# Packed attention and two mixtures of experts: two of four etm copies in batches 1 to 3 on VectorE

## The chip, the cores and the metric

One core of one Trainium2 chip runs the whole program in one launch. The metric is the device time in microseconds, the median of three runs. All stage times in this document are microseconds from the start of one profiled execution's span.

## What is computed

The reference, cut to what matters (S = 576 tokens, 4 batches, 8 heads, 32 packed queries, head width 64):

```python
def sm_attn(qq, kk, vv):
    s = scale * np.matmul(qq, kk.transpose(0, 1, 3, 2))
    a = np.exp(s - np.max(s, axis=-1, keepdims=True))
    a = a / (np.sum(a, axis=-1, keepdims=True) + 1e-09)
    return np.matmul(a, vv)

p_packed = sm_attn(p, k, v)                  # 32 packed queries read all tokens
out = sm_attn(q, p_packed, p_packed)         # the tokens read the 32 results
x = out.transpose(0, 2, 1, 3).reshape(2304, 512)

p = domain_probs / domain_probs.sum(-1)      # first mixture, 4 experts
x = sum(p[:, e:e+1] * (np.maximum(x @ w1[e], 0) @ w2[e]) for e in range(4))

logits = x @ phi                             # second mixture, 8 experts of 4 slots
d = softmax(logits, axis=0); slot_input = d.T @ x
slot_out = relu(slot_input @ w1) @ w2        # per expert
result = softmax(logits, axis=1) @ slot_out
```

## The kernel before

The program has three stages. A **head** loads and attends batch 0 and prepares the projected weights. The **main loop** makes 128 steps ("slots"), 32 for each batch; a slot multiplies one expert's 128 hidden features by all 576 tokens of its batch. The **tail** does the second mixture; it streams weights from memory.

Inside the main loop, the first-mixture work of batch b runs with the attention of batch b+1 threaded between. In each slot the kernel calls its steps in a fixed order written out by hand, "FGMLSAP": turn the hidden tile of the slot before (`flip_h`), make the next merged weights (`make_g`), multiply (`mm1`), take logits, one step of the softmax generator, one step of each attention generator, and the accumulations of the batch before. The engines run their own queues in this order; semaphores between them set the rest.

The attention of one batch is two generators, group 0 and group 1 of four heads each; group 1 starts nine slots after group 0 (`OFF1`). Each `yield` in `attention` ends its part of a slot. The steps around the change:

- L332 to L334: VectorE normalizes the exponentials `ex` of the packed scores (128 partitions by 576 tokens) and turns them by 32 by 32 blocks into `et`, where each of four heads has 32 partitions and each token block of 32 has 32 columns.
- L337 to L344: for each half of the token blocks (nine of eighteen), four copies bring `et` into the **block form** `etm`. Head h goes to its own 32 partitions, to parity h % 2, and into columns 0 to 31 or 32 to 63 of each 64-wide row; the other half of every row stays zero, so that one product serves two heads. The source is one run of 288 values per partition, the destination nine rows of 32 at a pitch of 64.
- L348 to L357, one slot later: TensorE multiplies the token blocks of v by `etm`, 18 matmuls per half (the trace has two records for each), parity 0 and parity 1 in turn, into the accumulator `pv`. Parity 0 reads the copies of heads 0 and 2, parity 1 those of heads 1 and 3.
- L361: ScalarE moves `pv` to `gl`, GpSimd spreads it to `pkt` (L370), and the second attention (`sb`, L381) reads `pkt`.

There is one `etm` buffer in the main loop. So the second half's copies wait for the first half's products. Per batch there are four sets of four copies, called here **g0h0, g0h1, g1h0, g1h1** (group, half); batches 1 to 3 have twelve sets, 48 copies.

What else stands in the queues near them: ScalarE drains each half of a hidden tile from PSUM with a Relu (L481, `ht`), and the merged weights by a cast (L458). VectorE turns the hidden tile (L487, `hn`) and makes the low part of the merged weights (L459), whose end frees the PSUM bank that the next product takes. GpSimd multiplies the turned tile by the domain probabilities (L488), multiplies in the attention softmax (L390, L399), makes low parts (L414) and issues the loads of q, k, v and p (L136, L143). Four PSUM banks serve `h`, `g`, `sa`, `sb` and `pv` in turn (`mm_ps`).

Of the kernel before, what the change touches and what calls it, by code (L numbers as in the profile page):

```python
# [18 lines left out]
def tile_packed_attention_moe_softmoe(  # L19
# [15 lines left out]
    pe, act, dve, pool, sp = nc.tensor, nc.scalar, nc.vector, nc.gpsimd, nc.sync  # L35
# [60 lines left out]
    def mm_ps(name, keep=None):  # L96
        i = (turns["mm"] + 1) % 4
        while i in kept.values():
            i = (i + 1) % 4
        turns["mm"] = i  # L100
        if keep is not None:
            kept[keep] = i
        return ps_mm[i].tile([128, 512], F32, tag="mm", name=name)
# [178 lines left out]
    def attention(b, g, feeds, ptb, pkb, etb, tmp, gp):  # L282
# [3 lines left out]
        def feed(key):  # L286
            if key in feeds:
                due.append(feeds[key])
# [48 lines left out]
        for hf in range(2):  # L337
            for h in range(4):
                r = slice(32 * h, 32 * h + 32)
                act.copy(  # L340
                    etb[hf % len(etb)][r, h % 2, :, 32 * (h // 2) : 32 * (h // 2) + 32],
                    et[r, HB * hf : HB * hf + HB, :],
                )
            yield  # L344
            vn = qkv_t.pop(("v", b, g, hf))
            if pv is None:
                pv = mm_ps(f"pv{bg}", bg)
            for x in range(HB):  # L348
                for par in range(2):
                    pe.matmul(  # L350
                        pv[64 * par : 64 * par + 64, :64],
                        vn[:, x, :],
                        etb[hf % len(etb)][:, par, x, :],
                        start=(hf == 0 and x == 0),
                        stop=(hf == 1 and x == HB - 1),
                        tile_position=(0, 64 * par),
                    )  # L357
            feed(f"k{hf}")
            if hf == 0:
                yield  # L360
# [59 lines left out]
    def start_attention(b, g):  # L420
        feeds = {}
        nb, ng = (b, 1) if g == 0 else (b + 1, 0)

        def later(src, nm, hf, bb, gg):
            return lambda: load_half(src, nm, bb, gg, hf)

        for hf in range(2):
            feeds[f"q{hf}"] = later(q, "q", hf, b, g)
            if nb < NB:
                feeds[f"k{hf}"] = later(k, "k", hf, nb, ng)  # L430
                feeds[f"v{hf}"] = later(v, "v", hf, nb, ng)
        if nb < NB:
            f = feeds["k0"]
            feeds["k0"] = lambda: (load_p(nb, ng), f())
        return attention(b, g, feeds, pt, pkt[:, g], [etm], att_tmp, pool)
# [335 lines left out]
    with tc.manual_schedule():  # L771
# [58 lines left out]
        def head_tmp(tag, name):  # L830
            if tag == "kt":
                return ht_pool.tile([128, S], F32, tag="ht", name=name)
            return spare[tag]

        gens = {
            "0": attention(0, 0, {}, pt, pkt[:, 0], [etm, et_x[0]], att_tmp, dve),
            "1": attention(
                0, 1, {}, pp1, pkt[:, 1], [et1, et_x[1]], head_tmp,
                pool if GP1 == "pool" else dve,
# [38 lines left out]
        for sl in range(nslot + 1):  # L878
# [3 lines left out]
            b, i = divmod(n, NU)  # L882
# [250 lines left out]
        for so, (d0, dw) in zip(sos, PARTS):  # L1133
            project(1, CHUNK // dw, dw, [(so, 0, dw)])
            h = slice(d0, d0 + dw)
# [56 lines left out]
```

## Time and profile before

| | |
|---|---|
| median of three runs | 533.5 us (532.25 to 533.76) |
| the profiled execution's own time | 533.42 us |
| its span in the trace | 531.6 us |
| TensorE, busy in the span | 493.3 us (93%) |
| VectorE, ScalarE, GpSimd, busy | 292.7, 236.0, 248.3 us |
| the 48 copies on ScalarE, one | 0.428 us |

Read it as follows. The profile's chain of waits goes back from the last instruction through whatever ended last. Its shares tell where a change of engine can matter. The timeline shows, for one stretch, each engine's instructions merged by group: start, length, engine, line, tile, count, and in square brackets how long the engine sat idle before the group and what ended that. An idle time of TensorE inside the main loop is time that the program could lose; an idle time of the other engines is not.

### The profile page before, as it was taken

How to read it: one execution, taken by the hardware profiler on the slowest of the kernel's cores; microseconds unless marked ns; L12 is line 12 of the kernel's file. 1: busy time of each engine (PE TensorE's matmuls, PEld its weight loads, DVE VectorE, ACT ScalarE, POOL GpSimd, SP SyncE). 2: the span in 40 equal slices, each digit the busy share in tenths (PEclk: the TensorE clock that was granted, in tenths of full speed). 3: DMA queues.
4: the chain of work that ended last, by engine and by line, in shares of the span. 5: the costliest groups of instructions: out<-in, count | busy, mean ns of one | idle time of the engine just before them, and what ended most of it. 6: DMA issues, size and time to landing. Idle time of an engine off the chain costs nothing.

```text
span 531.6 us, 12920 instructions
## 1 busy us (share of the span) xinstructions
PE 493.3 (93%) x5404; PEld 349.0 (66%) x5404; DVE 292.7 (55%) x539; ACT 236.0 (44%) x539; POOL 248.3 (47%) x310
## 2 busy tenths in 40 slices
PE   6898999999999999999999999999999987998883
PEld 5776877778765677787557778865678864323232
DVE  6265566656677656567775755676554553412031
ACT  3847555664552447465424474652355430111031
POOL 8502356487752367875326567842455540300000
PEclk9899999999999999999999999999999998898996
DMA  8999135433440353443304423443359449999998
GB/s 276 367 373 315 46 103 191 161 126 127 140 144 3 106 190 105 148 157 104 104 1 150 146 82 129 150 170 109 121 187 390 173 167 373 408 408 407 373 317 282
DMA packets 66713, 104.06 MB, mean 196 GB/s; under 512 B 4368, under 2 KB 50192, under 8 KB 66656
## 3 DMA queue, kind: packets, MB, share of 16 engines
q1 hardware_dynamic: 62640, 93.10, 49.5%
q0 software_dynamic: 3232, 9.75, 6.0%
q8 instruction: 42, 0.69, 0.5%
q10 hardware_dynamic: 784, 0.39, 0.3%
q14 instruction: 15, 0.12, 0.1%
HBM read 98.52 MB, written 4.72 MB: 194 GB/s over the span
## 4 chain that ended last, share of the span: by engine, by line
PE 66%; DMA 11%; DVE 8%; ACT 8%; issue 3%; POOL 3%; SPq 1%; POOLq 0%; DVEq 0%; ACTq 0%
PE h L477 32%; PE sl L648 7%; PE lg L504 6%; PE g L447 5%; DMA ck<-in_moe_w_dram 5%; DMA hn<-in_moe_w_dram 3%; ACT etm L340 3%; PE pv L350 3%; PE sb L301 3%; PE sa L301 2%; DMA k<-in_k_dram 2%; PE w2t L255 1%; PE si L1027 1%; PE o L1153 1%; POOL hn L488 1%
## 5 line engine op out<-in xcount | busy, mean ns | idle before, releaser
L477 PE MATMUL h<-a,g 128*128 128x288 f32 x1536 | 226.2, 302 | 2.5 <-POOL a L414 1.6
L477 PEld LDWEIGHTS h<-a,g 128*128 128x128 f32 x1536 | 208.0, 188 | 28.3 <-issue 22.3
L488 POOL TENSOR_TENSOR hn<-hn,dp_sb 128x576 f32<-128x576 f32 x128 | 151.5, 1190 | 123.0 <-DVE hn L487 118.7
L481 ACT ACTIVATE ht<-h 128x288 f32<-128x288 f32 x256 | 103.7, 412 | 149.4 <-PE h L477 149.0
L487 DVE STREAM_TRANSPOSE hn<-ht 128x576 f32<-128x576 f32 x128 | 96.6, 760 | 55.1 <-ACT ht L481 55.0
L459 DVE TENSOR_TENSOR g<-g,g 128x512 fp32r<-128x512 f32 x64 | 41.1, 684 | 26.5 <-ACT g L458 26.5
L648 PE MATMUL sl<-hn,dpt 32*32 32x512 f32 x1152 | 48.1, 597 | 1.5 <-DVE dpt L607 1.2
L458 ACT CAST g<-g 128x512 fp32r<-128x512 f32 x64 | 34.3, 588 | 21.0 <-PE g L447 21.0
L504 PE MATMUL lg<-ht,wphi 128*32 128x288 f32 x512 | 37.8, 412 | 0.0
L447 PE MATMUL g<-w,gl 64*32 64x512 f32 x512 | 35.7, 601 | 0.2 <-DVE tacc L666 0.2
L648 PEld LDWEIGHTS sl<-hn,dpt 32*32 32x32 f32 x1152 | 21.0, 103 | 21.5 <-issue 11.1
L504 PEld LDWEIGHTS lg<-ht,wphi 128*32 128x32 f32 x512 | 13.5, 109 | 32.7 <-issue 25.5
L350 PE MATMUL pv<-etm,v 128*64 128x64 f32 x468 | 20.0, 232 | 7.1 <-ACT etm L340 4.0
L414 POOL TENSOR_TENSOR a<-a,a 64x576 fp32r<-64x576 f32 x14 | 19.9, 1425 | 9.6 <-ACT a L413 8.9
L350 PEld LDWEIGHTS pv<-etm,v 128*64 128x64 f32 x468 | 17.1, 144 | 11.1 <-ACT etm L340 5.7
L340 ACT COPY etm<-et 32x288 f32<-32x288 f32 x52 | 22.2, 428 | 2.4 <-DVE et L334 1.2
L1120 PE MATMUL so<-hn,tacc 128*32 128x384 f32 (+1 forms) x96 | 19.5, 487 | 2.5 <-DMA hn<-in_moe_w_dram 2.4
L382 DVE STREAM_TRANSPOSE nat<-sb 128x288 f32<-128x288 f32 x14 | 6.8, 483 | 25.4 <-PE sb L301 25.4
L255 PE MATMUL w2t<-ident,hn 128*128 128x128 f32 x128 | 19.3, 301 | 1.4 <-ACT hn L260 1.4
L666 DVE TENSOR_TENSOR tacc<-sl,tacc 128x512 f32<-128x512 f32 (+2 forms) x32 | 15.3, 544 | 9.4 <-PE sl L648 9.4
L260 ACT COPY hn<-w2t 128x512 f32<-128x512 f32 x32 | 17.4, 588 | 6.8 <-PE w2t L255 6.8
L255 PEld LDWEIGHTS w2t<-ident,hn 128*128 128x128 f32 x128 | 15.8, 154 | 5.9 <-ACT hn L260 3.8
(179 smaller groups left out, 483.6 us busy)
## 6 DMA issues: line engine op xcount, KB each, us to landing
w<-in_moe_w_dram SPq DMA_DIRECT2D x32, 1024.0 KB, 5.3
ck<-in_moe_w_dram SPq DMA_DIRECT2D x44, 512.0 KB, 8.9
hn<-in_moe_w_dram SPq DMA_DIRECT2D x40, 512.0 KB, 9.9
hn<-in_moe_w_dram SPq DMA_DIRECT2D x16, 384.0 KB, 8.4
q<-in_q_dram POOLq DMA_DIRECT2D x12, 288.0 KB, 3.2
k<-in_k_dram POOLq DMA_DIRECT2D x10, 288.0 KB, 3.3
v<-in_v_dram POOLq DMA_DIRECT2D x10, 288.0 KB, 3.2
out_dram<-ob SPq DMA_DIRECT2D x7, 384.0 KB, 4.4
```

The costliest lines, as they stand in the source:

```text
L255: pe.transpose(ps[:, 128 * dc : 128 * dc + 128], w2_row(ft, e)[:, 128 * dc : 128 * dc + 128], ident,)
L340: act.copy(etb[hf % len(etb)][r, h % 2, :, 32 * (h // 2) : 32 * (h // 2) + 32], et[r, HB * hf : HB * hf + HB, :],)
L350: pe.matmul(pv[64 * par : 64 * par + 64, :64], vn[:, x, :], etb[hf % len(etb)][:, par, x, :], start=(hf == 0 and x == 0), stop=(hf == 1 an ...
L447: pe.matmul(pss[g][32 * ((c + 2 * g) % 4) : 32 * ((c + 2 * g) % 4) + 32, :], gl[b % 2][r, c, :], t[r, c], start=True, stop=True, tile_posi ...
L458: act.copy(hi, pss[g])
L459: dve.tensor_tensor(out=lo, in0=pss[g], in1=hi.bitcast(F32), op=ALU.subtract)
L477: pe.matmul(ps[:, :HS], gg[:, l, g, e % 2, fs], r[:, ts], start=(g == 0 and t == 0), stop=(g == 1 and t == 2),)
L481: act.activation(out=ht[:, ts], in_=ps[:, :HS], func=AF.Relu)
L487: dve.transpose(out=own, in_=unturned.pop((n, kf, e)).rearrange("p (x t) -> p x t", t=32))
L488: pool.tensor_tensor(out=own, in0=own, in1=dp_sb[:, n // NU, :, e].unsqueeze(2).to_broadcast([128, NBLK, 32]), op=ALU.mult,)
L504: pe.matmul(lg_t[b, pr][32 * c : 32 * c + 32, :HS], wphi[:, 2 * i + kf, 32 * e : 32 * e + 32], ht_t[n, kf, e][:, HS * hf : HS * hf + HS], ...
L648: pe.matmul(pss[f][c : c + 32, :], dpt[r, x, :], hn[r, p0 : p0 + NU, x, 2 * ep : 2 * ep + 2].rearrange("p n e k f -> p n (e k f)"), start= ...
```

## The change

Heads 2 and 3 of every set go to VectorE in batches 1 to 3. Batch 0, in the head, keeps all its copies on ScalarE. Nothing else is edited: 24 copies move, none is added.

```diff
         for hf in range(2):
             for h in range(4):
                 r = slice(32 * h, 32 * h + 32)
-                act.copy(
+                (dve.tensor_copy if b and h > 1 else act.copy)(
                     etb[hf % len(etb)][r, h % 2, :, 32 * (h // 2) : 32 * (h // 2) + 32],
                     et[r, HB * hf : HB * hf + HB, :],
                 )
```

On VectorE, batch 1, group 1, first half (g1h0): `et` is the turned softmax, `hn<-ht` the hidden tiles of two slots, `g` the low part of the merged weights.

```order
 L334 STREAM_TRANSPOSE et_1328<-ex_1190 128x576 [waits DVE_49]
 L487 STREAM_TRANSPOSE hn<-ht_1_2_1305 128x18x32 [waits Activation_49]
+L340 COPY etm<-et_1328 32x9x32 [waits DVE_49]
+L340 COPY etm<-et_1328 32x9x32
 L487 STREAM_TRANSPOSE hn<-ht_1_3_1332 128x18x32 [waits Activation_49]
 L459 TENSOR_TENSOR g_1_1356<-g_1_0_1357,g_1_1356 128x512 [waits Activation_49]
```

Two copies now stand between the two hidden-tile transposes, and ahead of the low part of the weights.

On VectorE, the same batch and group, second half (g1h1): `a` is the turned result of group 0's second softmax.

```order
 L487 STREAM_TRANSPOSE hn<-ht_0_0_1379 128x18x32 [waits DMAHW6_49,DMAHW5_49,DMAHW7_49,DMAHW0_49,Activation_49]
 L404 STREAM_TRANSPOSE a_1444<-nat_1268 128x576 [waits Pool_49]
+L340 COPY etm<-et_1328 32x9x32 [waits PE_49] x2
 L487 STREAM_TRANSPOSE hn<-ht_0_1_1427 128x18x32 [waits Activation_49]
 L487 STREAM_TRANSPOSE hn<-ht_1_0_1452 128x18x32 [waits Activation_49]
```

The two copies stand behind a transpose that waits for GpSimd, and wait themselves for TensorE, which must have finished the first half's products.

On ScalarE, the set g1h0 again: `nat` is the exponential of group 0's second softmax, `g` the cast of the merged weights.

```order
 L394 ACTIVATE nat_1268<-nat_1268 128x576 [waits Pool_49]
 L340 COPY etm<-et_1328 32x9x32 [waits DVE_49]
-L340 COPY etm<-et_1328 32x9x32 x3
+L340 COPY etm<-et_1328 32x9x32
 L458 CAST g_1_1356<-g_1_0_1357 128x512 [waits PE_49]
 L458 CAST g_1_1356<-g_1_1_1358 128x512 [waits PE_49]
```

Two copies instead of four stand ahead of the two casts.

## Rows read from the trace of the kernel before

**Rows 1.** The page's chain that ended last, share of the span by line
```profile
PE h L477 32%; PE sl L648 7%; PE lg L504 6%; PE g L447 5%; DMA ck<-in_moe_w_dram 5%; DMA hn<-in_moe_w_dram 3%; ACT etm L340 3%; PE pv L350 3%; PE sb L301 3%; PE sa L301 2%; DMA k<-in_k_dram 2%; PE w2t L255 1%; PE si L1027 1%; PE o L1153 1%; POOL hn L488 1%
```

**Rows 2.** Timeline (start, length, work, [idle before <- releaser]), batch 1, g0h1
```profile
78.67 1.29 DVE L459 TENSOR_TENSOR g<-g,g 128x512 fp32r<-128x512 f32 x2 [1.49 <-ACT g L458]
79.00 3.45 PE L477 MATMUL h<-a,g 128*128 128x288 f32 x24
...
81.33 1.79 ACT L340 COPY etm<-et 32x288 f32<-32x288 f32 x4
...
82.72 1.71 PE L350 MATMUL pv<-etm,v 128*64 128x64 f32 x36 [0.27 <-ACT etm L340]
```

**Rows 3.** Timeline, batch 1, g1h0
```profile
101.06 1.40 DVE L487 STREAM_TRANSPOSE hn<-ht 128x576 f32<-128x576 f32 x2
...
101.96 1.77 ACT L340 COPY etm<-et 32x288 f32<-32x288 f32 x4
...
102.80 1.86 PE L477 MATMUL h<-a,g 128*128 128x288 f32 x12
103.76 1.07 ACT L458 CAST g<-g 128x512 fp32r<-128x512 f32 x2
104.38 1.29 DVE L459 TENSOR_TENSOR g<-g,g 128x512 fp32r<-128x512 f32 x2 [1.92 <-ACT g L458]
...
105.12 1.27 PE L350 MATMUL pv<-etm,v 128*64 128x64 f32 x36 [0.46 <-DVE g L459]
```

**Rows 4.** Timeline, batch 1, g1h1
```profile
106.32 3.45 PE L477 MATMUL h<-a,g 128*128 128x288 f32 x24
...
108.17 0.78 DVE L404 STREAM_TRANSPOSE a<-nat 128x576 f32<-128x576 f32 x1 [0.62 <-POOL nat L399]
...
108.66 1.79 ACT L340 COPY etm<-et 32x288 f32<-32x288 f32 x4
...
110.05 1.71 PE L350 MATMUL pv<-etm,v 128*64 128x64 f32 x36 [0.28 <-ACT etm L340]
```

**Rows 5.** Timeline, batch 1, g0h0
```profile
68.22 6.64 PE L477 MATMUL h<-a,g 128*128 128x288 f32 x48
...
73.73 1.40 DVE L487 STREAM_TRANSPOSE hn<-ht 128x576 f32<-128x576 f32 x2
73.84 1.79 ACT L340 COPY etm<-et 32x288 f32<-32x288 f32 x4
74.54 2.33 POOL L488 TENSOR_TENSOR hn<-hn,dp_sb 128x576 f32<-128x576 f32 x2 [1.87 <-DVE hn L487]
...
75.23 1.71 PE L350 MATMUL pv<-etm,v 128*64 128x64 f32 x36 [0.37 <-ACT etm L340]
```

**Rows 6.** Timeline, group 0's scores in batch 2, and the same place in batch 3
```profile
188.99 0.78 DVE L292 STREAM_TRANSPOSE k<-k 128x576 f32<-128x576 f32 x1 [2.14 <-DMA k<-in_k_dram]
...
189.91 1.21 PE L301 MATMUL sa<-k,pt 128*128 128x288 f32 x4 [0.47 <-ACT ht L481]
...
292.73 1.21 PE L301 MATMUL sa<-k,pt 128*128 128x288 f32 x4 [0.79 <-DVE k L292]
```

**Rows 7.** VectorE's groups by form: line, tiles, shapes, count, busy, mean ns
```profile
L186 DVE TENSOR_REDUCE dps<-dp_sb 128x72 f32<-128x288 f32 x1 | 0.5, 452 | 0.0
```

**Rows 8.** Timeline, GpSimd and VectorE before g0h0 of batch 1
```profile
71.49 1.19 POOL L488 TENSOR_TENSOR hn<-hn,dp_sb 128x576 f32<-128x576 f32 x1 [2.80 <-DVE sm L330]
...
71.70 1.29 DVE L332 TENSOR_SCALAR ex<-ex,sm 128x576 f32<-128x576 f32 x1
```

**Rows 9.** Timeline, batch 1, GpSimd's spread of pv and the product behind it
```profile
116.61 1.93 POOL L370 COPY pkt<-gl 32x32 f32<-32x32 f32 x8
...
118.89 1.13 PE L301 MATMUL sb<-q,pkt 128*128 128x288 f32 x4
```

**Rows 10.** The tail: SyncE's timeline, then a stretch (length, engines' busy, PEclk, DMA share, GB/s)
```profile
437.46 15.55 SPq L749 DMA_DIRECT2D hn<-in_moe_w_dram  x16
...
470.00:480.00 10.00, 10.00 (x76) 2.84 (x72) 2.05 (x4) 1.60 (x4) 0.00 (x0) 1.00 1.03 409
```

## The prediction

> **What bounds the kernel now.** I read the chain of waits first. TensorE's products carry most of it, but ScalarE's etm copies have 3% of it by themselves and pv, the product that reads them, another 3% [rows 1]. A copy that is on the chain is one that TensorE waits for. So the timeline around each of the twelve sets comes next, and in each I look at two things: when TensorE ends the work in front of pv, and when pv really flows. A pv that nothing holds takes 1.27 us for its 36 records [rows 3]. Where the fourth copy comes late it takes 1.71 [rows 2, 4, 5]: two records run after the third copy, and the other 34 after the fourth, so 0.44 us of that group is a hidden wait. The idle time in brackets and this 0.44 are together what a set costs TensorE.
>
> **The change, part by part.** *What moves.* Twelve sets give up two ScalarE copies each. Four take 1.79 us [rows 2], one 0.45, so two take 0.90 and heads 0 and 1 are ready 0.9 us earlier than the set is today. *The price on VectorE.* No row shows this copy there. [...] A copy that VectorE could do faster is bounded below by half the column rate: L332 shows 576 columns done 0.31 us after GpSimd's multiply ended (71.70 + 1.29 against 71.49 + 1.19) [rows 8], so 288 columns could take 0.16 to 0.31. I take 0.46, the row with the same column count and no wait in it, so 0.92 a pair. Upward the bound is a copy that must first wait for a whole GpSimd multiply of 1.19 us: 1.19 + 0.31 = 1.50, 3.0 a pair. No reason excludes it; it is a rival below.
>
> *g0h1, batch 1.* TensorE ends h at 79.00 + 3.45 = 82.45; pv starts 0.27 later and loses 0.44 inside, 0.71 in all [rows 2]. VectorE's copies stand right behind L459, which ends at 79.96, and their wait for the first half's product is long over: done by 80.88. ScalarE's two end at 81.33 + 0.90 = 82.23. Both are ahead of 82.45, so all **0.71** goes. What is late next is h itself.
>
> *g0h1, batches 2 and 3.* The same 0.71 appears there, but little of it lasts. Group 0's second score product needs the second half of k. In batch 2 its turned form is ready at 188.99 + 0.78 = 189.77, after a 2.14 us wait for the load, and sa starts at 189.91; so the shift ends at about **0.10** [rows 6]. In batch 3 sa already waits 0.79 us for that transpose: TensorE would only wait longer, **0** [rows 6]. The load hangs on the one before it, whose issue hangs on work ahead of this set, so the change doesn't move it. In batch 1 I let the gain stand: k there arrives early enough.
>
> *g1h0, three times.* Here pv waits 0.46 us not for the copies but for the PSUM bank that L459 frees; L459 waits for ScalarE's cast, and the cast for the four copies [rows 3]. With two copies gone the casts start 0.88 earlier, 102.88, and the first ends about 103.5. VectorE must be free by then: its first transpose ends about 101.8, two copies take it to 102.7, the second transpose to about 103.4. So L459's first half runs 103.5 to 104.2, and the bank is free before h ends at 102.80 + 1.86 = 104.66. pv follows h at once: **0.46** each. The cover that hides the added 0.92 on VectorE is its old idle time of 1.92 us before L459; a pair beyond 1.8 us would give the whole gain back (101.8 + 1.8 + 0.75 + 0.70 = 105.05). Queued behind the copies are the second transpose and with it GpSimd's next multiply, about 0.5 us later than today; what GpSimd does next waits for sums behind L459, which come earlier.
>
> *g1h1, three times.* h ends at 106.32 + 3.45 = 109.77, pv starts 0.28 later and loses 0.44: 0.72 [rows 4]. ScalarE's two copies end at 108.66 + 0.90 = 109.56. VectorE's stand behind L404, which ends 108.95 today, so 109.87 if nothing moved; but L404 waits for GpSimd's L399, which waits for sums behind L459, and L459 is 0.85 earlier by the step before. TensorE's own frame is 0.46 earlier, so the pair ends about 0.3 before h does. **0.72** each. The pattern of these two sets reads alike in batches 1, 2 and 3.
>
> *g0h0.* In batch 1, h ends at 74.86, pv loses 0.37 + 0.44 = 0.81 [rows 5]. VectorE's copies stand behind a transpose that ends about 74.47, so the last ends at 75.39, against 75.64 for ScalarE's fourth today: pv flows at 75.41 in place of 75.68, **0.27**. In batches 2 and 3 the accumulation of the batch before stands between copies and pv, so the copies are ready long before, and VectorE waits for TensorE there: **0**, and nothing lost.
>
> *Sum:* 0.27 + 0.71 + 0.10 + 3 x (0.46 + 0.72) = 4.62 us.
>
> *Does it reach the end?* The tail is bound by weight loads: 1.03 of the DMA engines' time at 409 GB/s. SyncE issues the long run of loads from 437.46, as the last accumulations of the main loop free their buffers [rows 10]. So the stream starts earlier by what TensorE gains, with the same bytes behind it, and I carry the gain through in full. Against the profiled execution, 533.42 - 4.62 = 528.8 us. That execution lies 0.08 below the median of the runs, so no correction.
>
> [...] L332 shows VectorE standing still until GpSimd's multiply ends, at 72.68, and then doing 576 columns in 0.31 us [rows 8]. [...]
>
> **The rivals.**
>
> *Copies and multiplies exclude each other.* As mechanism of this kernel: VectorE's first copy gets in, GpSimd's multiply goes next, the second copy waits 1.19 us for it. In g0h0 of batch 1 the multiply starts at 74.54, when the copies do [rows 5]: the second ends at about 76.2, a loss of 0.5. In g1h0 L459 slips to about 104.15 and pv to 104.9: 0.22 left. In g1h1 about 0.5 is left. In g0h1 GpSimd is idle or done in time. So -0.5 + 0.71 + 0.10 + 3 x 0.72 = 2.5, 530.9 us. For it: L332. Against: it needs the faster form of the copy. 0.15.
>
> *GpSimd becomes late.* After g1h1, sb needs pkt, which GpSimd ends at 118.54, and sb starts at 118.89 [rows 9]. If GpSimd's queue doesn't move up, only 0.35 of group 1's 1.18 stays, and with batches 2 and 3 taken like batch 1: 0.27 + 0.71 + 0.10 + 3 x 0.35 = 2.1, 531.3 us. Against: that queue waits, two steps before, for a ScalarE cast that itself stands behind the copies. 0.10.
>
> *Slower.* Each of the two copies waits for a multiply, 3.0 us a pair. Then g0h0 of batch 1 loses 1.8; g0h1 gains about 0.3; in g1h0 L459 slips past its old time by 1.1, and g1h1's copies, behind it, come 2.6 late in all: -1.8 + 0.3 - 3 x 2.6 = -9.3, 542.7 us. It decides from about 1.7 us a pair, 0.85 a copy, where the losses in group 1 and g0h0 pass the gain of g0h1. For it: VectorE is the busier engine of the two. Against: GpSimd has one multiply per slot, and no two free ones for one pair. 0.06.
>
> *It does not do what it says:* the gaps close, but another wait of TensorE opens by as much before the loads start, and under 1.6 us is left, near 532.5. For it: batches 2 and 3 already show one such place. 0.07. *More than forecast:* copies near 0.3 us and no exclusion give g0h0 of batch 1 its whole 0.81, and the k loads of batches 2 and 3 come forward; 4.62 + 0.54 + 0.6 + 0.7 = 6.5, 526.9 us. 0.07.
>
> **How the numbers follow.** The forecast has 0.55; its own range is 527.9 to 529.8, from pairs between 0.4 and 1.2 us. The range from 527.2 to 532.0 takes in the two rivals near 531 and leaves out the slower case and parts of the last two. About 0.3%, 1.6 us, is what a measurement of this kernel can tell from no change. Faster by more: 0.55 + 0.07 + 0.11 + 0.08 = 0.81. Within: 0.07 and what is left of the two middle rivals, 0.13. Slower: 0.06.
>
> **What would show it.** Right: etm on VectorE at about 0.46 us; in the six group 1 sets and g0h1 pv in one run of about 1.27 us with little idle before it; L459 of g1h0 about 0.9 earlier against the h in front of it; sa of batch 3 waiting longer for k, about 1.5 us; the hn loads of the tail issued near 432.9. Wrong: VectorE copies over 0.85 us, or a copy that ends when a GpSimd multiply does; pv still in 1.71; sb waiting for pkt; a tail that starts earlier and ends when it did.

## The result and the profile after

The changed kernel takes 527.86 us (median of 4, 526.99 to 529.14) where the kernel before took 532.88 in the same comparison (4, 531.61 to 533.76): a ratio of 0.9916, with a 95% interval from 0.9889 to 0.9942. A second comparison, on another chip, gave 528.46 against 532.12, 0.9930 [0.9908, 0.9952]. Forecast were 528.8 us and a gain of 4.62 us; the profiled execution of after took 528.35 us, 5.07 below that of before (533.42). The forecast holds. Times and gains below are in us.

The page's chain by line no longer names the copies, which had 3% [rows 1]; pv has gone from 3% to 2%, and the load of k from 2% to 4%:

```profile
PE h L477 35%; DMA hn<-in_moe_w_dram 7%; PE lg L504 6%; DMA ck<-in_moe_w_dram 6%; PE g L447 6%; PE sl L648 5%; DMA k<-in_k_dram 4%; PE sb L301 3%; PE sa L301 2%; PE pv L350 2%; PE w2t L255 1%; PE o L1153 1%; PE pw L241 1%; DVE tacc L666 1%; POOL hn L488 1%
```

The copies of after by engine, batches 1 to 3 (count, shortest/median/longest in ns, first and last start), and who waited for them:

```profile
L340 ACT COPY etm<-et x24: 413/432/432, 73.7 to 308.5; 32x288 f32<-32x288 f32 x24
L340 DVE COPY etm<-et x24: 444/447/451, 74.4 to 308.4; 32x288 f32<-32x288 f32 x24
...
  PEld pv L350: 1.4, 7
  PE pv L350: 0.2, 1
```

A copy takes 0.447 us on VectorE, with 7 ns between the shortest and the longest. Asked the same way, the trace of before has TensorE waiting 2.0 us for copies, 7 times, and its weight loads 5.5 us, 14 times; in after it is 0.2 us once, and 1.4 us 7 times.

The timeline of after at the four sets of batch 1 (start, length, work, idle before and releaser), in the order g0h0, g0h1, g1h0, g1h1, and then the spread of pv and the product behind it; it answers to [rows 2 to 5] and [rows 9]:

```profile
74.37 0.92 DVE L340 COPY etm<-et 32x288 f32<-32x288 f32 x2
74.42 1.19 POOL L488 TENSOR_TENSOR hn<-hn,dp_sb 128x576 f32<-128x576 f32 x1 [1.87 <-DVE hn L487]
...
74.96 0.30 PE L350 MATMUL pv<-etm,v 128*64 128x64 f32 x2 [0.23 <-DVE etm L340]
...
75.44 1.23 PE L350 MATMUL pv<-etm,v 128*64 128x64 f32 x34 [0.18 <-ACT ht L481]
...
78.73 3.46 PE L477 MATMUL h<-a,g 128*128 128x288 f32 x24
79.72 0.92 DVE L340 COPY etm<-et 32x288 f32<-32x288 f32 x2
...
82.11 1.27 PE L350 MATMUL pv<-etm,v 128*64 128x64 f32 x36
...
100.79 0.91 DVE L340 COPY etm<-et 32x288 f32<-32x288 f32 x2
100.84 1.19 POOL L488 TENSOR_TENSOR hn<-hn,dp_sb 128x576 f32<-128x576 f32 x1 [0.54 <-DVE hn L487]
...
101.75 1.86 PE L477 MATMUL h<-a,g 128*128 128x288 f32 x12
...
102.44 1.29 DVE L459 TENSOR_TENSOR g<-g,g 128x512 fp32r<-128x512 f32 x2
...
103.55 1.27 PE L350 MATMUL pv<-etm,v 128*64 128x64 f32 x36
104.75 3.44 PE L477 MATMUL h<-a,g 128*128 128x288 f32 x24
...
107.05 0.93 DVE L340 COPY etm<-et 32x288 f32<-32x288 f32 x2
...
108.12 1.27 PE L350 MATMUL pv<-etm,v 128*64 128x64 f32 x36
...
114.64 1.94 POOL L370 COPY pkt<-gl 32x32 f32<-32x32 f32 x8
...
116.52 1.13 PE L301 MATMUL sb<-q,pkt 128*128 128x288 f32 x4
```

In g0h1, g1h0 and g1h1 all 36 records of pv run in 1.27 us with no bracket: no idle time that the profile shows stands before them. In g1h0 L459 starts 0.69 after h does (102.44 against 101.75), where it was 1.58 in before (104.38 against 102.80 [rows 3]), 0.89 earlier against it. Only g0h0 still runs in two pieces, 2 and 34. GpSimd's eight copies of the spread end at 116.58 (the profile's spans of GpSimd are rough) and sb starts without idle time at 116.52, where it started 0.35 after their end [rows 9]: GpSimd came forward by 1.96, TensorE by 2.37, and sb does not wait for it. The 0.35 to spare there are used up.

The timeline of after where group 1's second score product needs k, in batches 2 and 3; it answers to [rows 6], whose products are group 1's too and not group 0's, as their heading has it. In batch 3 the two lines of SPq and POOL ahead are SyncE's load of w, the factors of the next merged weights, and GpSimd's issue of the first part of k; the second part is issued at 284.79:

```profile
186.48 0.78 DVE L292 STREAM_TRANSPOSE k<-k 128x576 f32<-128x576 f32 x1 [2.02 <-DMA k<-in_k_dram]
...
187.41 1.21 PE L301 MATMUL sa<-k,pt 128*128 128x288 f32 x4 [1.08 <-DVE k L292]
...
277.05 14.46 SPq L169 DMA_DIRECT2D w<-in_moe_w_dram  x2
277.51 0.54 POOL L143 DMA_DIRECT2D k<-in_k_dram  x1
283.71 0.78 DVE L292 STREAM_TRANSPOSE k<-k 128x576 f32<-128x576 f32 x1 [1.76 <-DMA k<-in_k_dram]
...
284.79 0.58 POOL L143 DMA_DIRECT2D k<-in_k_dram  x1 [2.44 <-DVE k L292]
...
287.86 0.78 DVE L292 STREAM_TRANSPOSE k<-k 128x576 f32<-128x576 f32 x1 [2.06 <-DMA k<-in_k_dram]
...
288.79 1.21 PE L301 MATMUL sa<-k,pt 128*128 128x288 f32 x4 [1.41 <-DVE k L292]
```

TensorE waits 1.08 and 1.41 us there, against 0.47 and 0.79 [rows 6]. The first part of k, issued at 277.51, 0.46 behind a 1 MB load of w, is turned at 283.71, 6.2 us later; the second part's issue waits for that (2.44).

SyncE's timeline in the tail, and a stretch of it (length, busy time of TensorE, its weight loads, VectorE, ScalarE and GpSimd, granted clock of TensorE, DMA share, GB/s); it answers to [rows 10]:

```profile
432.21 14.35 SPq L749 DMA_DIRECT2D hn<-in_moe_w_dram  x16
...
465.00:475.00 10.00, 10.00 (x76) 2.84 (x72) 2.06 (x4) 1.60 (x4) 0.00 (x0) 1.00 1.03 410
```

The stream of loads starts 5.25 earlier than in before and runs at 410 GB/s, where it was 409, and the execution takes 5.07 less.

### The profile page after: what moved, and what is told of

Its sections match the earlier page's. It is cut to its first block, busy times and chain, and to the rows that moved or that the text cites. A ratio compares the mean times of both kernels' runs of the same rounds, so it can differ in the third digit from the quotient of the medians.

```text
span 526.6 us, 12931 instructions
## 1 busy us (share of the span) xinstructions
PE 490.3 (93%) x5404; PEld 347.9 (66%) x5404; DVE 303.9 (58%) x563; ACT 226.4 (43%) x515; POOL 248.4 (47%) x310
## 4 chain that ended last, share of the span: by engine, by line
PE 65%; DMA 17%; DVE 7%; issue 4%; ACT 4%; POOL 2%; SPq 1%; POOLq 0%; DVEq 0%; ACTq 0%
PE h L477 35%; DMA hn<-in_moe_w_dram 7%; PE lg L504 6%; DMA ck<-in_moe_w_dram 6%; PE g L447 6%; PE sl L648 5%; DMA k<-in_k_dram 4%; PE sb L301 3%; PE sa L301 2%; PE pv L350 2%; PE w2t L255 1%; PE o L1153 1%; PE pw L241 1%; DVE tacc L666 1%; POOL hn L488 1%
## 5 line engine op out<-in xcount | busy, mean ns | idle before, releaser
L459 DVE TENSOR_TENSOR g<-g,g 128x512 fp32r<-128x512 f32 x64 | 41.1, 685 | 20.6 <-ACT g L458 20.6
L301 PE MATMUL sa<-k,pt 128*128 128x288 f32 x56 | 17.2, 434 | 3.0 <-DVE k L292 2.9
L350 PE MATMUL pv<-etm,v 128*64 128x64 f32 x468 | 17.1, 225 | 2.6 <-ACT etm L340 1.3
L350 PEld LDWEIGHTS pv<-etm,v 128*64 128x64 f32 x468 | 15.1, 138 | 5.1 <-issue 2.0
```

What stands on the lines that cost most here:

```text
L301: pe.matmul(ps[:, :HS], lhs[:, j, :], t[:, :, j, :], start=(j == 0), stop=(j == 1))
L350: pe.matmul(pv[64 * par : 64 * par + 64, :64], vn[:, x, :], etb[hf % len(etb)][:, par, x, :], start=(hf == 0 and x == 0), stop=(hf == 1 an ...
L459: dve.tensor_tensor(out=lo, in0=pss[g], in1=hi.bitcast(F32), op=ALU.subtract)
```

## How the stages are compared

The head does not take the same time in every execution: group 0's second score product of batch 1, which stands ahead of every moved copy in the loop, starts between 61.47 and 63.44 in the fourteen profiles of this study. In the six where it starts at 63.25 to 63.44, those of before and after among them, TensorE's granted clock in the stretch from 51 to 56 is 0.66 (in before it is 0.50 from 53 to 55, in after from 52 to 54); in the other eight it is 1.00, and the product starts at 61.47 to 62.30. The stretch in after and in the kernel with group 1 alone (columns as in the tail above):

```profile
51.00:56.00 5.00, 4.95 (x26) 4.48 (x27) 4.76 (x17) 2.58 (x5) 0.34 (x1) 0.66 0.21 74
51.00:56.00 5.00, 4.76 (x44) 4.29 (x46) 4.48 (x16) 3.47 (x8) 0.59 (x1) 1.00 0.18 60
```

Just ahead of it TensorE waits twice for GpSimd, about 0.7 and 0.8, in all fourteen, and the runs do not show why the clock falls in some. It stands ahead of the change, and single times scatter by it: with nearly the same start ahead of the stretch (a product at 49.56 in after, 49.59 with one copy of four) the mark came at 63.31 and 61.98. So I count all stages from that product ("the mark"; 63.44 in before, 63.31 in after), and give for each place how much earlier it is than in the profile of before. The places are the last second-attention product of batches 1 to 3 ("end of batch", behind all four sets), the two score products of group 1 between them, and the first hn load of the tail in [rows 10] ("loop end"). g0h0 and g0h1 lie ahead of the first score product, k's wait between the two, group 1's sets behind the second. A later number in a row minus the one before it is what the stage between them gained.

| kernel | b1 end | b2 sa 1 | b2 sa 2 | b2 end | b3 sa 1 | b3 sa 2 | b3 end | loop end |
|---|---|---|---|---|---|---|---|---|
| after | 2.23 | 2.97 | 2.37 | 3.69 | 4.46 | 3.81 | 5.15 | 5.12 |
| after, second profile | 1.89 | 2.64 | 1.81 | 3.12 | 3.88 | 2.42 | 2.18 | 2.16 |
| group 1 alone | 1.32 | 1.30 | 1.40 | 2.72 | 2.70 | 2.06 | 3.39 | 3.37 |
| group 0 alone | 0.79 | 1.53 | 0.66 | 0.63 | 1.39 | 0.28 | -1.34 | -1.36 |
| group 0 alone, second profile | 0.84 | 1.60 | 0.72 | 0.70 | 1.47 | 0.82 | 0.84 | 0.85 |
| one copy of four | 1.76 | 2.17 | 1.89 | 2.77 | 3.17 | 2.64 | 3.56 | 3.56 |
| four of four | -0.32 | 0.48 | 0.09 | -0.01 | 0.92 | 0.78 | 0.77 | 0.75 |
| two, done twice | -1.18 | -0.44 | -1.25 | -1.76 | -0.99 | -1.70 | -2.20 | -2.21 |
| two, in two pieces each | -0.89 | -0.17 | -0.91 | -1.48 | -0.74 | -1.76 | -1.11 | -1.12 |
| before + later w | 0.00 | -0.03 | 0.60 | 0.70 | 0.68 | 1.64 | 1.74 | 1.73 |
| group 0 + later w | 0.72 | 1.48 | 2.12 | 2.11 | 2.89 | 3.25 | 3.26 | 3.29 |
| after + later w | 2.13 | 2.88 | 3.44 | 4.50 | 5.24 | 5.25 | 6.60 | 6.58 |
| after + later w, second profile | 2.23 | 3.01 | 3.63 | 4.11 | 4.88 | 5.19 | 6.54 | 6.52 |

## Experiments

The theory to be tested: a set costs TensorE the time by which its fourth copy comes late, and two copies on each engine remove that; group 1's gain lasts, and group 0's is mostly given back at k. The rivals were those of the prediction.

**Which group brings it.** Group 1 alone, then group 0 alone; the edits are against after, as in all experiments but one.

```diff
-                (dve.tensor_copy if b and h > 1 else act.copy)(
+                (dve.tensor_copy if b and g and h > 1 else act.copy)(
```

> Only the sets of group 1 give heads 2 and 3 to VectorE; group 0 keeps four copies on ScalarE. If each set costs TensorE what its fourth copy is late, the gain is that of group 1 in the trace of the changed kernel, three times 0.53 and 0.80, 4.0 us against the kernel before, near 528.9. Rival: the gain comes from a ScalarE that is less busy altogether; half the copies then give half the gain, 2.5 us, near 530.4.

Measured: 528.09 us (6 runs, 527.33 to 529.39), ratio to before 0.9916 [0.9897, 0.9935]. Each batch's group 1 gives 1.32 to 1.33 in the table, 4.0 in all; 0.64 is lost at k in batch 3 (sa 1 to sa 2), so 3.37 stay at the loop's end. Group 0's copies can't be the cause of that loss, since they did not move here: k's two parts were turned 6.27 and 3.79 after their issues, where before took 6.00 and 3.40. The rival that counts copies (2.5) is out.

```diff
-                (dve.tensor_copy if b and h > 1 else act.copy)(
+                (dve.tensor_copy if b and not g and h > 1 else act.copy)(
```

> Only the sets of group 0 give heads 2 and 3 to VectorE. By the late fourth copy and the wait for k behind it: 0.16 + 0.75 in batch 1, 0.15 in batch 2 and 0.12 in batch 3, 1.2 us, near 531.7. By the rival, half of the whole gain: 2.5 us, near 530.4. If the wait for k did not take the gain of batches 2 and 3: 0.16 + 3 x 0.75 = 2.4 us.

Measured: 532.22 us (12 runs, 530.34 to 534.40), 0.9995 [0.9978, 1.0013], no difference that can be told. The sets do gain: 0.79 is there at the end of batch 1, and 0.74 and 0.76 are added in the next two (from the end of one batch to sa 1 of the next), but 0.87 and 1.11 are lost between sa 1 and sa 2: more than the set of the same batch had brought. The excess is k itself: from issue to turning its two parts took 0.12 longer than in before in batch 2 and 0.34 longer in batch 3. 1.2 and a time near 531.7 were expected. And in batch 3 another 1.62 goes behind sa 2. The timeline there, and the stretch behind the wait (columns as in the tail above):

```profile
290.73 1.21 PE L301 MATMUL sa<-k,pt 128*128 128x288 f32 x4 [1.91 <-DVE k L292]
...
291.87 1.86 PE L447 MATMUL g<-w,gl 64*32 64x512 f32 x16
...
293.66 2.04 PE L504 MATMUL lg<-ht,wphi 128*32 128x288 f32 x16
...
291.80:295.60 3.80, 3.80 (x33) 0.77 (x32) 1.97 (x4) 1.47 (x3) 2.59 (x3) 0.55 0.78 238
```

After the wait of 1.91 us TensorE's granted clock is 0.55 over the next 3.8 us; g and lg take 1.86 and 2.04, where in after they take 1.09 and 1.18 at a granted clock of 1.00. To see whether every wait for k does that, the kernel was profiled again.

> The kernel with only group 0's copies split, a second profile. In its first profile TensorE waited 1.91 us for k in batch 3 and the granted clock was 0.55 in the 3.8 us behind it; the accumulated g and lg there took 1.86 and 2.04 us in place of 1.09 and 1.18. If that drop of the clock is what made that execution 2 us longer than the median's lower half (530.3 to 531.7), then a profile without the drop shows g at 1.09, lg at 1.18 and a time near 531.3. Rival: the drop follows every such wait in this kernel; then g and lg read 1.86 and 2.04 again and the time is near 534.

Measured: 533.21 us. TensorE waited 1.46 us, the next stretch had 1.00:

```profile
291.81 1.21 PE L301 MATMUL sa<-k,pt 128*128 128x288 f32 x4 [1.46 <-DVE k L292]
...
291.80:295.60 3.80, 3.79 (x40) 1.78 (x41) 2.70 (x5) 1.47 (x3) 3.71 (x6) 1.00 0.57 174
```

So the drop does not follow every such wait, and the loss is 1.6 us where it comes. The time I had expected, 531.3, was missed: the loop ended 0.85 earlier than in before, not 1.2, and this execution's mark is at 63.34, with the lower clock in the head, 1.62 later than the first one's. How much of the miss the head is worth the record doesn't show, since the executions near 531.3 were not profiled.

**Is the split the point, or the relief of ScalarE?** One copy of four on VectorE, then all four.

```diff
-                (dve.tensor_copy if b and h > 1 else act.copy)(
+                (dve.tensor_copy if b and h == 3 else act.copy)(
```

> One copy in place of two moves: head 3 to VectorE, three copies stay on ScalarE. By the late copy: ScalarE is 0.45 earlier and not 0.9, so g1h0 gains 0.45 (of 0.53), g1h1 and g0h1 keep a wait of about 0.25 for the third copy (0.53 and 0.50 gained), g0h0 of batch 1 gains 0.43: 0.43 + 0.50 + 0.27 + 3 x 0.98 = 4.1 us, near 528.8. By the rival that counts copies: 2.5 us, near 530.4.

Measured: 528.94 us (6 runs, 527.92 to 529.82), 0.9929 [0.9913, 0.9946]. Every set of batch 1 gains 0.41 to 0.46. In group 0's two, pv now runs in 1.27 but starts 0.37 and 0.28 late, as in before, behind ScalarE's third copy. One copy brings 3.56 of the 5.12 at the loop's end; 4.1 was expected, and 2.5 by the rival that counts copies.

```diff
-                (dve.tensor_copy if b and h > 1 else act.copy)(
+                (dve.tensor_copy if b else act.copy)(
```

> All four copies of each set in batches 1 to 3 go to VectorE, none to ScalarE. The set is then 1.8 us long on VectorE, as it was on ScalarE. By the late copy it should cost about what the kernel before costs: -0.6 in g0h0 of batch 1, +0.75 and +0.27 in g0h1 (VectorE starts earlier there), 0 to -0.2 in groups 1, near 533. Rival: what counts is relief of ScalarE, whose queue also holds the drains of the hidden tiles; then at least the gain of the changed kernel, 527.9 or less.

Measured: 531.91 us (12 runs, 530.98 to 533.38), 0.9988 [0.9975, 1.0002]. A queue of four on VectorE takes as long as one of four on ScalarE (1.77 to 1.86 us in batch 1), and TensorE waits for it in place of the other. The timeline of this kernel, g0h0 and g1h0 of batch 1:

```profile
72.55 1.83 DVE L340 COPY etm<-et 32x288 f32<-32x288 f32 x4
...
74.05 1.65 PE L350 MATMUL pv<-etm,v 128*64 128x64 f32 x36 [1.02 <-DVE etm L340]
...
103.31 1.27 PE L350 MATMUL pv<-etm,v 128*64 128x64 f32 x36 [0.27 <-DVE g L459]
```

ScalarE is relieved of twice as much, and 0.75 of the 5.12 is left at the loop's end. What counts is that two engines work on one set at the same time.

**Where the gain ends: a dearer pair.** VectorE makes each of its copies twice, into the same place.

```diff
-                (dve.tensor_copy if b and h > 1 else act.copy)(
+                for _ in range(2 if b and h > 1 else 1):
+                    (dve.tensor_copy if b and h > 1 else act.copy)(
```

> As the changed kernel, but VectorE makes each of its copies twice (the same values to the same place), so a pair costs 1.8 us and not 0.9; ScalarE as in the changed kernel. The prediction put the break-even near 1.7 us a pair: -0.6 in g0h0 of batch 1, +0.75 and +0.27 in g0h1, about -0.2 in each group 1, so within 1 us of the kernel before, near 533; pv should wait for VectorE in groups 1. Rival: VectorE has idle time enough (58% busy), the extra 22 us of copies cost nothing, and 527.9 stays.

Measured: 536.07 us (6 runs, 535.33 to 539.29), 1.0072 [1.0048, 1.0097]. A pair takes 1.87 to 1.89. In batch 1 g0h0 loses 0.80, g1h0 0.09 and g1h1 0.49, g0h1 brings 0.76, and the wait for k takes another 0.5 to 0.8 in each batch. This is the slower rival: 3.6 us in the medians with a pair of 1.88, where 9.3 was worked out for a pair of 3.0. Between a pair of 0.92 (5.12 gained) and one of 1.88 (2.21 lost), a straight line crosses zero at 0.92 + 0.96 x 5.12 / 7.33 = 1.59 us; by the medians (5.0 gained, 3.6 lost) at 0.92 + 0.96 x 5.0 / 8.6 = 1.48. So, estimated from these two, it decides near 1.5 us a pair, not 1.7; that the loss grows in a straight line between them is assumed, and no run lies there. Within 1 us of before was expected for this kernel.

**Do copies and GpSimd's multiplies exclude each other?** The same two copies in two pieces each, eight rows and one row; the question is whether this form is faster alone and then has to wait for a multiply that it meets.

```diff
-                (dve.tensor_copy if b and h > 1 else act.copy)(
-                    etb[hf % len(etb)][r, h % 2, :, 32 * (h // 2) : 32 * (h // 2) + 32],
-                    et[r, HB * hf : HB * hf + HB, :],
-                )
+                for x0, x1 in ((0, 8), (8, 9)) if b and h > 1 else ((0, HB),):
+                    (dve.tensor_copy if b and h > 1 else act.copy)(
+                        etb[hf % len(etb)][r, h % 2, x0:x1, 32 * (h // 2) : 32 * (h // 2) + 32],
+                        et[r, HB * hf + x0 : HB * hf + x1, :],
+                    )
```

> As the changed kernel, but each VectorE copy is cut in two: eight token blocks (source one run of 256, destination 8 rows) and the ninth alone, so that the outermost counts of source and destination are both even. [...] If the form does not depend on the counts, 0.42 and 0.18 us with little spread whatever GpSimd does, 1.2 us a pair, and 528 to 528.5.

Measured: 533.39 us (12 runs, 532.64 to 535.22), 1.0017 [1.0004, 1.0029], above the 529 to 531 that were expected for a form that is faster and waits. The copies of this kernel by engine, then its timeline at g0h0, g0h1 and g1h0 of batch 1; the line at 72.88 is the second of the four pieces that the line at 72.67 sums up:

```profile
L341 DVE COPY etm<-et x48: 166/286/1582, 72.7 to 313.4; 32x256 f32<-32x256 f32 x24, 32x32 f32<-32x32 f32 x24
...
72.67 1.78 DVE L341 COPY etm<-et 32x256 f32<-32x256 f32 x4
72.72 1.28 POOL L489 TENSOR_TENSOR hn<-hn,dp_sb 128x576 f32<-128x576 f32 x1 [1.87 <-DVE hn L488]
...
72.88 1.15 DVE L341 COPY etm<-et 32x32 f32<-32x32 f32 x1
...
74.50 1.23 PE L351 MATMUL pv<-etm,v 128*64 128x64 f32 x34 [1.10 <-DVE etm L341]
...
78.78 0.79 DVE L341 COPY etm<-et 32x256 f32<-32x256 f32 x4
...
100.31 1.76 DVE L341 COPY etm<-et 32x256 f32<-32x256 f32 x4
100.36 1.28 POOL L489 TENSOR_TENSOR hn<-hn,dp_sb 128x576 f32<-128x576 f32 x1 [0.53 <-DVE hn L488]
```

Four pieces take 0.79 us when GpSimd is idle (78.78), so this form is faster than the copy of nine rows, whose pair took 0.92. When a multiply starts beside them the same four take 1.76 to 1.78. The piece that waits there is the second, one row of 32: it starts while the multiply runs and ends 0.03 after it (72.88 + 1.15 against 72.72 + 1.28), where it takes 0.17 alone. A piece of eight rows can wait too: in g1h1 one that starts at 107.37 takes 1.58, until 0.15 after a multiply that ends at 108.80, where it takes 0.28 alone. The copies of after, at 74.37 and 100.79 with a multiply 0.05 behind, took 0.92 and 0.91. So the exclusion is there in these runs, and it goes with the form of the copy, not with the operation: the pieces have it, the copies of nine rows don't. It is the rival of the prediction, and dearer than worked out there: 533.39 measured, 530.9 forecast for it. What in the shapes makes the difference is not shown; only these two forms were run.

**What group 0's gain is lost to.** The w load of one expert pair, which SyncE issues 0.46 us ahead of k's first part (277.05 and 277.51), is issued three slots later and from ScalarE's queue, in the two slots in which it stood beside the loads of k for batches 2 and 3. First on after, then on before. Time and queue of that load change together here; no run tells them apart.

```diff
-    def load_w1():
+    def load_w1(eng=sp):
...
-        sp.dma_start(
+        eng.dma_start(
...
-        due.append(load_w1)
+        if pr and n in (NU + 1, 2 * NU + 1):
+            late(3)
+        else:
+            due.append(load_w1)
+
+    def late(k):
+        due.append(lambda: late(k - 1) if k else load_w1(act))
```

> The changed kernel, and in batches 1 and 2 the one weight load of 1 MB that starts just ahead of the k load of the next group (178.4 and 280.9 in the trace before) is issued from ScalarE's queue three slots later. If that load is why k takes 5.8 us to land there and 3.1 elsewhere, k and the scores come 2.7 us earlier, and TensorE's waits of 1.08 and 1.41 us for the turned k in the changed kernel go: 2.3 us less, near 525.6. If k is slow for another reason: 527.9. If the weights then come too late for their product, a wait on the load shows at TensorE and the time rises above 528.

Measured: 526.64 us (5 runs, 525.96 to 527.98), 0.9886 [0.9868, 0.9905]. The timeline of this kernel at the same place of batch 3:

```profile
276.66 0.54 POOL L143 DMA_DIRECT2D k<-in_k_dram  x1
281.13 0.78 DVE L292 STREAM_TRANSPOSE k<-k 128x576 f32<-128x576 f32 x1
...
287.29 1.21 PE L301 MATMUL sa<-k,pt 128*128 128x288 f32 x4 [0.79 <-DVE k L292]
```

The first part of k is turned without a wait, 4.5 us after its issue in place of 6.2. In batch 2 TensorE no longer waits for k, in batch 3 0.79 in place of 1.41. The loop ends 1.46 earlier than in after; I had expected more, and batch 3's second part of k and a w that comes 0.19 late for g in batch 2 (0.84 in the second profile) take part of the rest.

> The same late weight load on the kernel before, without the change. TensorE's waits at the same two scores are 0.47 and 0.79 us there, so at most 1.0 to 1.3 us less than before, near 531.7. With the run of the changed kernel that has it, this tells whether the two steps add (then 5.0 + 1.1) or the late load gives back what the wait for k took from group 0's sets (then 5.0 + 2.3).

Measured: 530.64 us (12 runs, 529.56 to 532.29), 0.9968 [0.9954, 0.9982]. The same edit on before, with all copies on ScalarE, gains 1.73 at the loop's end, nearly all of it at sa 2 of batches 2 and 3. At most 1.0 to 1.3 was expected, from the waits of 0.47 and 0.79 there; the gains at sa 2 are 0.63 and 0.96. The two steps nearly add: 5.12 + 1.73 = 6.85, and together they gave 6.58. With the later load as the ground, group 0's split was tried again:

> Only group 0's copies split, together with the w load of two slots put three slots later (as in the earlier run on the kernel before, 530.64). Theory, the k load eats group 0's gain: with k in time g0h0 of batch 1 gives 0.16 and the three g0h1 0.75 each, 2.4 in all beside what the later load gives, so near 528.3 us, and the second score product of group 1 waits for k by under 0.5 us in batches 2 and 3. Rival, group 0's sets are worth nothing for another reason: 530.6, as without them.

Measured: 528.70 us (4 runs, 528.18 to 528.95), 0.9930 [0.9910, 0.9950], 1.9 us below the later load without the split by the medians, and 1.5 if each is taken against the kernel before on its own chip; the loop ends differ by 1.56. Its two second score products in batches 2 and 3:

```profile
185.82 1.21 PE L301 MATMUL sa<-k,pt 128*128 128x288 f32 x4
...
287.51 1.21 PE L301 MATMUL sa<-k,pt 128*128 128x288 f32 x4 [0.45 <-ACT ht L487]
```

The same edit that was worth nothing by itself is worth 1.5 to 1.9 us when k comes sooner. Group 0's sets gain, and the wait for k is what takes it: in batch 2, with no wait left, the whole gain passes sa 2. In batch 3 k is still late (0.45), and about 0.6 of 0.78 is lost there against the later load without the split; so 1.56 came in place of the 2.4 expected.

**Side by side.** After, and after with the later load, on one chip.

> The changed kernel again, on the same chip as the next run, for a direct comparison: 527.9 us.

> The changed kernel with the w load of two slots put three slots later, again beside the changed kernel: 526.6 us, 1.2 less than it. Rival, the first difference was chance: within 0.4 of it.

Measured: 528.46 us (6 runs, 526.95 to 531.15) and 525.71 (4 runs, 525.40 to 526.85; 0.9879 [0.9861, 0.9897] to before). The ranges do not meet; the medians are 2.75 apart, in the first pair of comparisons, on different chips, they were 1.2. So the later load is worth 1.2 to 2.75 us on top, 1.46 by the first two loop ends, and the version with both beats both kernels. Part of the larger number is the lower clock again: the profiled execution of after is its slowest here (531.15), and its timeline and stretch at batch 3 read

```profile
290.15 1.47 PE L301 MATMUL sa<-k,pt 128*128 128x288 f32 x4 [2.16 <-DVE k L292]
...
291.55 1.96 PE L447 MATMUL g<-w,gl 64*32 64x512 f32 x16
...
291.50:295.00 3.50, 3.50 (x34) 0.76 (x33) 1.27 (x3) 1.48 (x3) 2.31 (x3) 0.59 0.67 204
```

With k that late (2.16 us) the clock fell once more, to 0.59, and the loop's gain is 2.16 in place of 5.12.

## Why the prediction was right, step by step

- **VectorE's price.** 0.46 was taken from a reduction with the same column count (0.452 [rows 7]); that a copy costs as much was the author's estimate, and 0.447 was measured. The choice between its bounds, 0.16 to 0.31 and 1.50, was right: all 24 copies took 0.444 to 0.451, with a multiply beside them or not, so there was no faster form and no exclusion. No row showed that beforehand; it was the author's estimate too. Both bounds are real for the other form: 0.28 for eight rows alone, 1.58 for eight rows that meet a multiply.
- **g1h0 and g1h1, 3 x (0.46 + 0.72).** Measured 0.53 and 0.80, the same in all three batches. Each is 0.07 to 0.08 larger than the wait that vanished. When nothing holds pv it starts 0.06 to 0.07 before the modelled end of h (108.12 against 104.75 + 3.44 = 108.19); the term counted from that end. The cover of g1h0, VectorE's idle time before L459, held as worked out: 102.44 is 0.69 behind h's start, forecast 0.70.
- **g0h1 of batch 1, 0.71.** Measured 0.75, by the first score product of group 1 (0.90 in all); the early start of 0.08 is there too (82.11 against 78.73 + 3.46), and ScalarE's drain of pv (a wait of 0.31 for gl ahead of the next h) stays as it was.
- **g0h0 of batch 1, 0.27.** Measured 0.15 (the g behind pv starts 13.29 after the mark, 13.44 in before). VectorE's pair ended as forecast (74.37 + 0.92 = 75.29, or 75.42 by before's mark; 75.39 was forecast). The 34 records started 0.15 after it, where the step had 0.02. The term was mis-sized by that gap between the last copy's end and the product. A like gap stood in the rows: in before, sa starts 0.14 after VectorE has turned k (188.99 + 0.78 against 189.91 [rows 6]), and in every profile it starts 0.15 after it where it waits for k. The gap is not the same everywhere: behind ScalarE's fourth copy in before (75.63 to 75.68), and behind VectorE's fourth in the kernel with four of four, it was 0.05. Why is open.
- **Batches 2 and 3 of group 0, 0.10 and 0.** 0.74 and 0.77 appear at sa 1, and 0.60 and 0.65 are given back at sa 2: 0.14 and 0.12 stay. The mechanism, k's load, was right and is shown by the later load. The 0.10 of batch 2 was luck: it was read as room between the turned k and sa, and that 0.14 is the gap that stands at every sa that waits for k, so no room was left. What stayed came from k, whose parts were turned 5.78 and 3.03 after their issues in place of 5.82 and 3.16. One name in that step was wrong: the product that waits is group 1's second score product, not group 0's (group 1 starts nine slots later). And batch 3 kept 0.12, not 0, again by k's landing: 6.20 and 3.07 (284.79 to 287.86) where before took 6.00 and 3.40. The wait of 1.41 was forecast as about 1.5.
- **The tail.** The sum of the measured terms is 0.15 + 0.75 + 0.14 + 0.12 + 3 x 1.33 = 5.15, the loop ends 5.12 earlier, and the two profiled times differ by 5.07. The one-to-one step through the load-bound tail holds for this pair, to 0.2: from that load to the end it is 94.37 in after and 94.16 in before. Over the fourteen profiles it is 94.15 to 95.5, so a single execution can't show it better. The loads start at 432.21 (432.9 forecast).
- **The rivals.** Exclusion is false for this copy (0.444 to 0.451), and true for the pieces of eight rows and of one (0.28 and 0.17 alone, up to 1.58 and 1.15 with a multiply): what was put against it, that it needs the faster form, held. GpSimd late is false: the spread came forward with the rest, and sb does not wait for it. The slower case exists, at a pair of 1.88 us; its point of decision was put at 1.7 and is near 1.5, and one reason is k's wait, which the step left out and which takes 0.5 to 0.8 a batch more. "More than forecast" named the k loads as what could come forward; they came forward with TensorE's own frame, and no further.

What the sum left out is what a k that lands later can do: in two of the fourteen profiles, where its two parts took 0.45 and 0.84 longer than in the other profile of the same kernel, the clock fell behind the wait, and 1.6 us more were lost. Why k lands later in some executions is not settled. Nor can the times tell whether group 0's split is worth anything in after itself: group 1 alone measured 528.09, both together 527.86 and 528.46, while the traces give group 0 1.2 by its terms, and 1.75 as the difference of the two loop ends (5.12 and 3.37).

## What to carry to other kernels

A product that reads four small copies waits for the last of them, so give two to an engine that is idle at that moment; the gain is at most the time of half the queue (here 0.9; the sets gained 0.16 to 0.80), and ends where the second engine's own successors become late (here, by estimate, near 1.5 us a pair, where 0.9 was spent). Follow each saved microsecond to the next thing that does not move with it, a load whose issue hangs on earlier work: there it ends, and there the next change is to be made. Before moving a copy beside a busy GpSimd, measure its form alone and beside a multiply: here the form that was faster alone (a pair 0.79 against 0.92) was the one that had to wait (1.76 to 1.78).

## What the runs showed of the hardware

- The same data copied by VectorE in nine rows of 32 took 0.444 to 0.451 us whether or not GpSimd multiplied beside it; in eight rows and one, two such copies took 0.79 us alone, and a single piece up to 1.58 us where it met a multiply.
- TensorE's granted clock fell behind waits of 1.91 and 2.16 us (0.55 and 0.59 in the next 3.5 to 3.8 us), and stayed at 1.00 behind waits of 1.41 and 1.46 at the same place; behind one of 1.82 (the kernel with the two pieces) g and lg took 1.09 and 1.18, as they do at 1.00. Where it fell, 1.6 us were lost beyond the wait itself. In the head it fell (0.66 from 51 to 56) in six of fourteen profiles behind two waits of 0.7 to 0.8 that stand in all.
- 288 KB of k, issued by GpSimd 0.46 us behind a 1 MB load, was turned 6.2 us after its issue, and 4.5 us after it when that load came later.
- Wherever sa waited for the turned k, it started 0.145 to 0.148 us after VectorE's end, and pv in g0h0 of after 0.15 behind each of VectorE's two copies. Behind the fourth copy in g0h0 of before (ScalarE) and of the kernel with four of four (VectorE) it started 0.05 after.
